# A new order for the first batch's transposes and scores, causal masks on VectorE, and the first v loaded by two queues

## The chip, the cores and the metric

The kernel runs on one core of one Trainium2 chip. The metric is the device time of one execution in microseconds (us). A core has the engines TensorE (PE, matmuls; its weight loads are shown apart as PEld), VectorE (DVE), ScalarE (ACT), GpSimd (POOL) and SyncE (SP), each with its own queue of instructions worked through in order. POOL and SP also issue DMAs.

## The reference

Attention with a decay that each key position carries, then a two-layer feed-forward net with exact GELU on the result.

```python
# q, k, v: (8, 8, 576, 64) float32 (batch, heads, positions, width); s: (8, 8, 576)
scores = scale * np.matmul(q, k.transpose(0, 1, 3, 2))
causal = np.triu(np.ones((S, S), dtype=bool), k=1)
s_pos = np.maximum(s, 0.0)
cum = np.cumsum(s_pos, axis=-1)
bias = -(cum[:, :, :, None] - cum[:, :, None, :])
scores = np.where(causal, -1000000000.0, scores + np.minimum(bias, 0.0))
scores = scores - np.max(scores, axis=-1, keepdims=True)
attn = np.exp(scores)
attn = attn / (np.sum(attn, axis=-1, keepdims=True) + 1e-09)
attn_out = np.matmul(attn, v)
x = attn_out.transpose(0, 2, 1, 3).reshape(B * S, H * D)      # (4608, 512)
h = x @ w_in                                                  # w_in (512, 2048)
out = (0.5 * h * (1.0 + erf(h / np.sqrt(2)))) @ w_out         # w_out (2048, 512)
```

## The kernel before

The work goes by batch b (8 of them, 8 heads each, taken as 4 pairs of heads) and by chunk c of 512 rows of the feed-forward net (9 of them). The scores are computed transposed, keys on the partitions. Since the decay splits into a factor of the key and one of the query, a key's factor (`wb`, an exp of `cum`) is multiplied into v once (`scale_v`, giving `vv`), and numerator and denominator are two matmuls against the same exponentials P.

All instructions of an engine are emitted in the order in which the code below calls them; no scheduler moves them. Waits between engines come from the tiles' reads and writes, and from the number of buffers of a tile. The items:

- `load_pair` issues the q or k of one pair of batch 0, with a cast to bf16, from POOL. `load_v` issues v (ten pieces for batch 0, in two halves of four heads), `load_w` the weights, `load_qk` q and k of a later batch, all from POOL. POOL lets at most eight DMAs be under way: a ninth waits for the first to land. The `pace` copies make POOL wait for a landing or for another engine before it issues more.
- `tr_item(b, p, i)` transposes q (i = 0) or k (i = 1) of a pair: 18 small PE transposes (L350) into one PSUM tile `tr_ps`, then one copy of it into `qkT` (L355), by DVE or, where given, by ACT.
- `sc_item(b, p)` makes the scores of a pair in two units. Each unit is some matmuls (L367) into `sc_ps` and one exp on ACT into P (L383). The causal mask comes in two ways. With `neg=True`, more matmuls add -2048 above the diagonal ahead of the exp (L375, operands `ident_bf` and `neg_bf`). Without it, `mask_item` multiplies P by a triangle of ones and zeros on DVE (L392, L397, operand `tri_bf`).
- `weights_scan`, `weights_dve`, `weights_pe` make `cum` (a scan on DVE, L246) and `wb` (five transposes on PE into `t_ps`, L255, then an exp on ACT).
- `scale_pair(0, p)` makes `vv` of a pair on DVE (L221, two instructions).
- `av_item` makes numerator and denominator of a pair (L405), and `norm` divides by way of ln and exp on ACT (L422, L423) and a product on DVE into `xT` (L438).
- `l1_item` (L486) and `l2_item` (L505) are the two layers.

For batches 0 and 1, q and k are transposed by PE. From batch 2 on DVE interleaves them (`interleave`), SP writes them to DRAM (`write_rows`) and reads them back through the DMA transpose (`transpose_rows`, L185). SP also stores the output (L514).

The prologue, which the change rewrites, works on batch 0. In the kernel before, pair 0 is transposed, then the q of pair 1, then the scores of pair 0; from then on the transposes of a pair come right ahead of its own scores. All four pairs are masked by PE. PE begins with nine matmuls on a tile of zeros (`warm`, L536), and POOL makes the identity after the loads of pair 0. After the prologue come the four `av_item` of batch 0, and then, with c = 0, the feed-forward net with the items of batch 1 between its matmuls.

Of the kernel before, what the change touches and what calls it, by code (L numbers as in the profile page):

```python
# [19 lines left out]
def kernel(  # L20
# [10 lines left out]
    nc = tc.nc  # L31
    fp32 = mybir.dt.float32
    bf16 = mybir.dt.bfloat16
    AF = mybir.ActivationFunctionType
    MULT = mybir.AluOpType.mult
    ALU = mybir.AluOpType
    AX = mybir.AxisListType.X

    B, H, S, D = q.shape
    scale = 1.0 / (D ** 0.5)  # L40
    BH = B * H
    ST = 5
    SL = S - 512
    NP = H // 2
# [38 lines left out]
    work = fast.enter_context(tc.tile_pool(name="work", bufs=1))  # L83
# [10 lines left out]
    early = {}  # L94
# [15 lines left out]
    def load_pair(b, n, p):  # L110
        src = q if n == "q" else k
        if p == 0:
            early[b, n] = work.tile([128, 2, 2, G * D], bf16, tag=f"raw{n}", bufs=3, name=f"early_{n}")
        e0 = (p // 2) * 64
        nc.gpsimd.dma_start(
            out=early[b, n][e0 : e0 + 64, p % 2],
            in_=bass.AP(
                tensor=src.tensor,
                offset=src.offset + (b * H + 2 * p) * S * D,
                ap=[[G * D, 64], [S * D, 2], [1, G * D]],  # L120
            ),
        )

    busy = const.tile([128, 512], bf16, name="busy")
    nc.vector.memset(busy, 0.0)
    for n in "qk":
        load_pair(0, n, 0)
    ident = const.tile([128, 128], fp32, name="ident")
    make_identity(nc, ident)
    for p in range(1, NP):  # L130
        for n in "qk":
            load_pair(0, n, p)
    uptri = const.tile([128, 128], fp32, name="uptri")
# [11 lines left out]
    neg_bf = const.tile([128, 128], bf16, name="neg_bf")  # L145
# [8 lines left out]
    raws = {}  # L154
# [29 lines left out]
        for i in range(2):  # L184
            nc.sync.dma_start_transpose(out=qkT[b % 2][:, i, p, :S], in_=rows_of[b, i][p % 2, p // 2])  # L185

    def load_v(b, h0=0, h1=H):
        if (b, "v") not in raws:
            raws[b, "v"] = work.tile([128, ST, H, D], fp32, tag="rawv", bufs=3, name="raw_v")
        t = raws[b, "v"]  # L190
        for st in range(ST):
            n_st = 128 if st < ST - 1 else SL
            nc.gpsimd.dma_start(  # L193
                out=t[:n_st, st, h0:h1, :],
                in_=bass.AP(
                    tensor=v.tensor,
                    offset=v.offset + (b * H + h0) * S * D + st * 128 * D,
                    ap=[[D, n_st], [S * D, h1 - h0], [1, D]],
                ),
            )  # L200
# [47 lines left out]
    def weights_dve():  # L248
        nc.vector.tensor_scalar(cum, s_pos, s_pos[:, 287:288], None, op0=ALU.subtract)
# [94 lines left out]
    def tr_item(b, p, i, copy=None):  # L344
        t_ps = ps.tile([128, G, 64], bf16, tag="av", bufs=3, name="tr_ps")
        e0 = (p // 2) * 64
        src = early[b, "qk"[i]]
        for r in range(G):
            for e in range(2):
                nc.tensor.transpose(  # L350
                    t_ps[e * 64 : e * 64 + 64, r, :],
                    src[e0 : e0 + 64, p % 2, e, r * D : (r + 1) * D],
                    ident_bf[e0 : e0 + 64, e0 : e0 + 64],
                )
        (copy or nc.vector.tensor_copy)(  # L355
            qkT[b % 2][:, i, p, :S].rearrange("d (g r) -> d g r", r=G), t_ps.rearrange("d r g -> d g r")
        )

    P_of = {}

    def sc_item(b, p, neg=False):
        P_of[b, p] = P = work.tile([128, 2, PW], bf16, tag="P", bufs=4, name="P")
        for u in range(NU):
            s_ps = ps.tile([128, 2, 512], fp32, tag="sc", bufs=2, name="sc_ps")
            for jt, i0, n, off in UNITS[u]:
                for e in range(2):
                    nc.tensor.matmul(  # L367
                        s_ps[:, e, off : off + n],
                        lhsT=qkT[b % 2][e * 64 : e * 64 + 64, 1, p, jt * 128 : jt * 128 + 128],
                        rhs=qkT[b % 2][e * 64 : e * 64 + 64, 0, p, i0 : i0 + n],  # L370
                        start=True, stop=not neg, skip_group_check=neg,
                    )
            for lo, n, w in ((0, 2, 128), (448, 1, 64))[: u + 1 if neg else 0]:
                for e in range(2):
                    nc.tensor.matmul(  # L375
                        s_ps[:, e, 0:512].rearrange("p (g c) -> p g c", c=256)[:, :, 0:128]
                        if n == 2 else s_ps[:, e, lo : lo + w],
                        lhsT=ident_bf,
                        rhs=neg_bf[:, :w].unsqueeze(1).to_broadcast([128, n, w])
                        if n == 2 else neg_bf[:, :w],  # L380
                        start=False, stop=True, skip_group_check=True,
                    )
            nc.scalar.activation(  # L383
                P[:, :, UO[u] : UO[u] + UW[u]], s_ps[:, :, : UW[u]], func=AF.Exp, scale=scale
            )
            if not neg:
                mask_item(b, p, u, nc.vector)

    def mask_item(b, p, u, eng):
        P = P_of[b, p]  # L390
        d = P[:, :, UO[u] : UO[u] + 512].rearrange("p e (g c) -> p e g c", c=256)[:, :, :, 0:128]
        eng.tensor_tensor(  # L392
            d, d, tri_bf.unsqueeze(1).unsqueeze(1).to_broadcast([128, 2, 2, 128]), op=MULT
        )
        if u == 1:
            d = P[:, :, UO[u] + 448 : UO[u] + 512]
            eng.tensor_tensor(  # L397
                d, d, tri_bf[:, :64].unsqueeze(1).to_broadcast([128, 2, 64]), op=MULT
            )
# [123 lines left out]
    def scale_pair(b, p):  # L523
        scale_v(b, ((0, ST - 1), (ST - 1, ST)), nc.vector, 2 * p, 2 * p + 2)

    for t in vv:
        nc.vector.memset(t[64:128, ST - 1, :, :], 0.0)
    make_upper_triangular(nc, uptri, 1.0, diag=True)
    load_v(0, 0, H // 2)
    load_v(0, H // 2, H)  # L530
    for i in range(4):
        load_w(0, i)
    weights_scan()
    warm = ps.tile([128, 2, 512], fp32, tag="sc", bufs=2, name="warm")
    for i in range(9):
        nc.tensor.matmul(warm[:, i % 2], lhsT=busy[:, :128], rhs=busy, start=True, stop=True)  # L536
    tr_item(0, 0, 0, nc.scalar.copy)
    tr_item(0, 0, 1)
    weights_dve()
    nc.vector.tensor_scalar(neg_bf, uptri, 2048.0, -2048.0, op0=MULT, op1=ALU.add)  # L540
    tr_item(0, 1, 0, nc.scalar.copy)
    sc_item(0, 0, neg=True)
    weights_pe()
    tr_item(0, 1, 1)
    sc_item(0, 1, neg=True)
    for p in (2, 3):
        tr_item(0, p, 0)
        tr_item(0, p, 1)
        sc_item(0, p, neg=True)
    nc.vector.tensor_copy(tri_bf, uptri)  # L550
    for p in range(NP):
        scale_pair(0, p)
    nc.gpsimd.memset(amv, 0.0)
    nc.gpsimd.memset(ones, 1.0)
    nc.gpsimd.memset(qkT[1][:, 1, :, S:640], 0.0)
# [121 lines left out]
    with tc.If(rv > 0):  # L677
        with tc.tile_pool(name="gen", bufs=1) as gen, tc.tile_pool(
            name="gps", bufs=1, space=bass.MemoryType.PSUM
# [20 lines left out]
            with tc.For_i(0, B, 1) as b:  # L700
# [8 lines left out]
                for h in range(H):  # L709
# [17 lines left out]
                    for it in range(ST):  # L727
# [27 lines left out]
                        h0 = h - e  # L755
# [68 lines left out]
```

## Time and profile before

| | |
|---|---|
| time, median of 9 runs | 341.92 us (340.9 to 343.35) |
| the profiled execution: its own time, its span | 342.64 us, 340.6 us |
| busy PE, DVE, ACT, POOL | 326.5, 192.5, 203.7, 68.0 us |
| DMA | 47.30 MB, mean 139 GB/s |
| scores of pair 0 start on PE | 8.25 us |
| scores of pair 3 start on PE | 21.74 us |
| first `av_item` starts on PE | 24.01 us |
| first matmul of `l1_item` | 28.82 us |
| first scores of batch 2 | 83.7 us |

The profile is of one execution. In a timeline line the columns are the start in us from the span's start, the duration, the engine, the line of the kernel and the operation, output and inputs, and how many instructions were merged; in brackets stands the engine's idle time just before and what ended it. POOLq and SPq are the instruction queues of those engines, and DMA issues appear on them. A waits line gives the waiting engine and line, what it waited for, and then the total, the number and the longest of the waits. A line of stretches gives, for PE, PEld, DVE, ACT and POOL, the busy time and the number of instructions, and then PEclk (the granted clock), the DMA engines' busy share and GB/s. A line of the chain of waits gives start, duration and what the time went to.

### The profile page before, as it was taken

The page shows a single profiled execution, that of the slowest core. Times are in us where ns is not written, and L with a number is a line of the kernel's source. Part 1 is how long each engine was busy: PE and PEld are TensorE (multiplying, and loading weights), DVE is VectorE, ACT ScalarE, POOL GpSimd, SP SyncE. Part 2 cuts the span into 40 slices and gives each one's busy share as a digit, 9 for nine tenths or more (in the row PEclk, how much of TensorE's full clock was granted, in tenths as well). Part 3 has the DMA queues.
Part 4 walks back from the last instruction along what each step waited for, and adds up shares of the span by engine and source line. Part 5 has one row for each costly group of instructions (what it writes and reads, how often), then busy time and mean ns, then how long its engine had stood idle before and what let it go on. Part 6 is the DMA issues. An engine that isn't in the chain of part 4 may idle for free.

```text
span 340.6 us, 6373 instructions
## 1 busy us (share of the span) xinstructions
PE 326.5 (96%) x2571; PEld 165.3 (49%) x2571; DVE 192.5 (57%) x380; ACT 203.7 (60%) x288; POOL 68.0 (20%) x106
## 2 busy tenths in 40 slices
PE   7889999999999999999999999999999999999992
PEld 3455455554554455445544555455545554444440
DVE  5256638999857655774578456935693455140020
ACT  3549635786767676667756865785578576204400
POOL 8962354410001810070008000500000000000000
PEclk9999999999999999999999999999999999999998
DMA  7899999999477998599688954615710100010011
GB/s 118 187 206 192 205 215 239 206 275 154 137 196 107 192 211 236 130 220 210 158 119 186 202 169 113 178 39 192 126 48 3 62 33 31 33 62 31 3 64 67
DMA packets 53764, 47.30 MB, mean 139 GB/s; under 512 B 31392, under 2 KB 43680, under 8 KB 53728
## 3 DMA queue, kind: packets, MB, share of 16 engines
q0 software_dynamic: 16016, 23.07, 36.8%
q1 hardware_dynamic: 37712, 23.75, 27.7%
q8 instruction: 22, 0.36, 0.4%
q14 instruction: 14, 0.11, 0.1%
HBM read 36.85 MB, written 16.52 MB: 157 GB/s over the span
## 4 chain that ended last, share of the span: by engine, by line
PE 90%; ACT 4%; DVE 2%; DMA 1%; issue 1%; POOL 0%; ACTq 0%; DVEq 0%; POOLq 0%
PE o_ps L505 37%; PE h_ps L486 34%; PE sc_ps L367 6%; PE avn L405 4%; PE avd L405 3%; ACT L492 2%; PE tr_ps L350 1%; PE avw L405 1%; PE sc_ps L375 1%; DMA early_q<-in_q_dram 1%; DVE qkT L355 1%; PE avr L405 1%; ACT gT L492 1%; ACT P L383 1%; PE t_ps L255 0%
## 5 line engine op out<-in xcount | busy, mean ns | idle before, releaser
L505 PE MATMUL o_ps<-w_out_r,gT 128*128 128x512 bf16 x576 | 133.2, 380 | 0.0
L486 PE MATMUL h_ps<-xT,w_in_r 128*128 128x512 bf16 x576 | 126.7, 379 | 1.4 <-ACT gT L492 1.2
L486 PEld LDWEIGHTS <-w_in_r 128*128 128x128 bf16 x576 | 56.2, 98 | 69.9 <-issue 2.9
L383 ACT ACTIVATE P<-sc_ps 128x1024 bf16<-128x1024 f32 x64 | 62.4, 1023 | 39.4 <-PE sc_ps L367 31.7
L505 PEld LDWEIGHTS <-gT 128*128 128x128 bf16 x576 | 52.9, 98 | 60.6
L492 ACT ACTIVATE gT<-h_ps 128x1024 bf16<-128x1024 f32 x54 | 54.4, 1024 | 41.5 <-PE h_ps L486 41.2
L512 DVE COPY o_sb<-o_ps 128x512 f32<-128x512 f32 x36 | 24.8, 688 | 57.3 <-PE o_ps L505 57.3
L392 DVE TENSOR_TENSOR P<-P,tri_bf 128x512 bf16<-128x512 bf16 x56 | 23.6, 425 | 40.1 <-ACT P L383 39.9
L204 DVE TENSOR_REDUCE amx<-qkT 128x2 f32<-128x1152 bf16 x32 | 40.9, 1337 | 0.0
L193 POOL DMA_DIRECT2D raw_v<-in_v_dram x45 | 37.0, 836 | 18.0 <-DMA w_out_r<-in_moe_w_out_dram 7.6
L438 DVE SCALAR_TENSOR_TENSOR xT<-avn,ln 128x256 bf16<-128x256 f32 (+3 forms) x64 | 21.7, 385 | 26.6 <-ACT ln L423 26.6
L367 PE MATMUL sc_ps<-qkT 64*128 64x256 bf16 (+2 forms) x320 | 23.4, 264 | 3.5 <-DVE qkT L355 2.9
L422 ACT ACTIVATE ln<-avd 128x256 f32<-128x256 f32 x56 | 18.6, 393 | 11.1 <-PE avd L405 11.1
L221 DVE TENSOR_TENSOR vv<-raw_v,wb 128x512 bf16<-128x512 f32 (+2 forms) x46 | 25.2, 612 | 0.0
L423 ACT ACTIVATE ln<-ln 128x512 f32<-128x512 f32 (+1 forms) x40 | 23.5, 589 | 1.3
L495 ACT ACTIVATE gT<-h_ps 128x512 bf16<-128x512 f32 x36 | 19.7, 604 | 6.3 <-PE h_ps L486 6.3
L211 DVE TENSOR_REDUCE amv<-raw_v 128x1 f32<-128x2048 f32 (+1 forms) x16 | 22.9, 1471 | 0.0
L367 PEld LDWEIGHTS <-qkT 64*128 64x128 bf16 x320 | 13.3, 96 | 19.5 <-issue 14.6
L405 PEld LDWEIGHTS <-vv 128*64 128x64 bf16 x384 | 17.4, 113 | 6.9 <-issue 3.4
L405 PEld LDWEIGHTS <-wb 128*64 128x64 bf16 x384 | 17.6, 114 | 0.2
L582 POOL CAST pace<-gT 128x1 f32<-128x1 bf16 x4 | 0.8, 199 | 78.5 <-ACT gT L492 78.5
L355 DVE COPY qkT<-tr_ps 128x576 bf16<-128x576 bf16 x14 | 9.9, 752 | 11.5 <-PE tr_ps L350 11.5
(90 smaller groups left out, 177.3 us busy)
## 6 DMA issues: line engine op xcount, KB each, us to landing
out_dram<-o_sb SPq DMA_DIRECT2D x36, 256.0 KB, 2.3
raw_v<-in_v_dram POOLq DMA_DIRECT2D x28, 256.0 KB, 8.4
rows<-qk_bf SPq DMA_DIRECT2D x12, 576.0 KB, 3.4
early_q<-in_q_dram POOLq DMA_DIRECT2D x14, 288.0 KB, 10.4
early_k<-in_k_dram POOLq DMA_DIRECT2D x14, 288.0 KB, 10.5
w_in_r<-in_moe_w_in_dram POOLq DMA_DIRECT2D x4, 512.0 KB, 8.2
w_out_r<-in_moe_w_out_dram POOLq DMA_DIRECT2D x4, 512.0 KB, 14.3
raw_v<-in_v_dram POOLq DMA_DIRECT2D x15, 128.0 KB, 4.8
```

The source lines that it names most:

```text
L193: nc.gpsimd.dma_start(out=t[:n_st, st, h0:h1, :], in_=bass.AP(tensor=v.tensor, offset=v.offset + (b * H + h0) * S * D + st * 128 * D, ap=[ ...
L204: nc.vector.tensor_reduce(amx[:, b * NP + p], qkT[b % 2][:, :, p, :S], axis=AX, op=ALU.max, apply_absolute_value=True)
L221: eng.tensor_tensor(vb[:n_st, st0:st1, h0:h1, :], t[:n_st, st0:st1, h0:h1, :], wb[:n_st, st0:st1, b * H + h0 : b * H + h1] .unsqueeze(3).t ...
L367: nc.tensor.matmul(s_ps[:, e, off : off + n], lhsT=qkT[b % 2][e * 64 : e * 64 + 64, 1, p, jt * 128 : jt * 128 + 128], rhs=qkT[b % 2][e * 6 ...
L383: nc.scalar.activation(P[:, :, UO[u] : UO[u] + UW[u]], s_ps[:, :, : UW[u]], func=AF.Exp, scale=scale)
L392: eng.tensor_tensor(d, d, tri_bf.unsqueeze(1).unsqueeze(1).to_broadcast([128, 2, 2, 128]), op=MULT)
L405: nc.tensor.matmul(out[e * 64 : e * 64 + 64, lo : lo + n], lhsT=(wb[:, jt, b * H + h : b * H + h + 1].to_broadcast([128, 64]) if den else ...
L423: nc.scalar.activation(ln[:, :w], ln[:, :w], func=AF.Exp, scale=-1.0)
L486: nc.tensor.matmul(h_of[c, f2][i], lhsT=w_in_r[:, ko, ft * 128 : (ft + 1) * 128], rhs=xT[:, ko, c * NB % XW : c * NB % XW + NB], start=(ko ...
L492: nc.scalar.activation(gT_of[c][:, f2 * 2 : f2 * 2 + 2, :], hh_of[c, f2], func=AF.Gelu)
L505: nc.tensor.matmul(o_ps, lhsT=gT[:, ft, sub * 128 : (sub + 1) * 128], rhs=w_out_r[:, ft, :], start=(ft == 0), stop=(ft == FT - 1),)
L512: nc.vector.tensor_copy(o_sb, o_ps)
```

## The change

The transposes of a pair are emitted ahead of the scores of the pair in front of it, so that the k of pair p + 1 and the q of pair p + 2 stand on PE between two score items. Pairs 0, 1 and 2 are no longer masked by matmuls: `mask_item` on DVE does it, after the last of the transposes' copies and between the scalings of v; pair 3 keeps `neg=True`. q and k of pair 1 are issued ahead of the identity, which moves the identity on POOL behind two more DMA issues. The first four heads of v are issued by SP, the others by POOL; a small POOL copy from `early_k` (pair 1) into the v tile stands ahead of both, so that v is issued after that k has landed. One of the nine warm-up matmuls goes, and `neg_bf` and `tri_bf` are made later on DVE.

```diff
-    for n in "qk":
-        load_pair(0, n, 0)
+    for p in (0, 1):
+        for n in "qk":
+            load_pair(0, n, p)
     ident = const.tile([128, 128], fp32, name="ident")
     make_identity(nc, ident)
-    for p in range(1, NP):
+    for p in (2, 3):
         for n in "qk":
             load_pair(0, n, p)
...
-    def load_v(b, h0=0, h1=H):
+    def v_tile(b):
+        raws[b, "v"] = work.tile([128, ST, H, D], fp32, tag="rawv", bufs=3, name="raw_v")
+
+    def load_v(b, h0=0, h1=H, eng=nc.gpsimd):
         if (b, "v") not in raws:
-            raws[b, "v"] = work.tile([128, ST, H, D], fp32, tag="rawv", bufs=3, name="raw_v")
+            v_tile(b)
...
-            nc.gpsimd.dma_start(
+            eng.dma_start(
...
-    def sc_item(b, p, neg=False):
+    def sc_item(b, p, neg=False, masks=True):
...
-            if not neg:
+            if masks and not neg:
                 mask_item(b, p, u, nc.vector)
...
-    load_v(0, 0, H // 2)
+    v_tile(0)
+    nc.gpsimd.tensor_copy(
+        raws[0, "v"][:64, :, 0, 0], early[0, "k"][:64, 1, 0, 0:1].to_broadcast([64, ST])
+    )
+    load_v(0, 0, H // 2, nc.sync)
     load_v(0, H // 2, H)
...
-    for i in range(9):
+    for i in range(8):
         nc.tensor.matmul(warm[:, i % 2], lhsT=busy[:, :128], rhs=busy, start=True, stop=True)
     tr_item(0, 0, 0, nc.scalar.copy)
     tr_item(0, 0, 1)
     weights_dve()
-    nc.vector.tensor_scalar(neg_bf, uptri, 2048.0, -2048.0, op0=MULT, op1=ALU.add)
     tr_item(0, 1, 0, nc.scalar.copy)
-    sc_item(0, 0, neg=True)
+    sc_item(0, 0, masks=False)
     weights_pe()
     tr_item(0, 1, 1)
-    sc_item(0, 1, neg=True)
-    for p in (2, 3):
-        tr_item(0, p, 0)
-        tr_item(0, p, 1)
-        sc_item(0, p, neg=True)
+    tr_item(0, 2, 0)
+    nc.vector.tensor_scalar(neg_bf, uptri, 2048.0, -2048.0, op0=MULT, op1=ALU.add)
+    sc_item(0, 1, masks=False)
+    tr_item(0, 2, 1)
+    tr_item(0, 3, 0)
     nc.vector.tensor_copy(tri_bf, uptri)
+    sc_item(0, 2, masks=False)
+    tr_item(0, 3, 1)
+    mask_item(0, 0, 0, nc.vector)
+    mask_item(0, 0, 1, nc.vector)
+    sc_item(0, 3, neg=True)
     for p in range(NP):
         scale_pair(0, p)
+        if p < 2:
+            mask_item(0, p + 1, 0, nc.vector)
+            mask_item(0, p + 1, 1, nc.vector)
```

## The prediction

> **What bounds the kernel now.** I read the page first, then the chain of waits for the first 45 us, the waits of TensorE (PE), the timeline of each engine there, and last the DMA landings.
>
> ```profile
> PE   7889999999999999999999999999999999999992
> PE 90%; ACT 4%; DVE 2%; DMA 1%; issue 1%; POOL 0%; ACTq 0%; DVEq 0%; POOLq 0%
> ```
>
> PE is the bound: 90% of the chain that ends last, and short of nine tenths only in the first three slices, some 25 us. From L1's start at 28.8 us on it hardly waits, so a microsecond taken from the prologue reaches the end, unless a later wait eats it. The timeline, PE alone:
>
> ```profile
> 8.25 0.61 PE L367 MATMUL sc_ps<-qkT 64*128 64x256 bf16 x4
> 8.79 0.61 PE L375 MATMUL sc_ps<-neg_bf,ident_bf 128*128 128x256 bf16 x2
> 9.33 0.61 PE L367 MATMUL sc_ps<-qkT 64*128 64x256 bf16 x6
> 9.87 0.72 PE L375 MATMUL sc_ps<-neg_bf,ident_bf 128*128 128x256 bf16 x4
> 10.52 0.79 PE L255 MATMUL t_ps<-ident,cum 64*128 64x64 f32 x5
> ...
> 15.05 0.69 PE L350 MATMUL tr_ps<-ident_bf,early_q 64*64 64x64 bf16 x18
> 15.55 0.67 PE L350 MATMUL tr_ps<-ident_bf,early_k 64*64 64x64 bf16 x18
> 17.26 0.61 PE L367 MATMUL sc_ps<-qkT 64*128 64x256 bf16 x4 [1.04 <-DVE qkT L355]
> ...
> 21.74 0.61 PE L367 MATMUL sc_ps<-qkT 64*128 64x256 bf16 x4 [1.04 <-DVE qkT L355]
> ...
> 24.01 0.96 PE L405 MATMUL avw<-P,vv 128*64 128x256 bf16 x8
> ```
>
> Two things are seen: masks (L375) cost as much PE time as scores, and PE stands still while DVE copies the transposes it needs next. The waits of PE and the chain add the wait for pair 1's q:
>
> ```profile
> PE sc_ps L367 <- DVE qkT L355: 2.9, 3, 1.0
> ...
> 3.13 4.46 DMA early_q<-in_q_dram
> ```
>
> The second limit is the loads (timeline, all engines):
>
> ```profile
> 7.25 7.23 POOL L193 DMA_DIRECT2D raw_v<-in_v_dram  x10
> ...
> 14.46 3.01 POOL L238 DMA_DIRECT2D w_in_r<-in_moe_w_in_dram  x4
> ```
>
> and, in the stretches of 2 us, the DMA share (last but one) falls while POOL issues without a pause:
>
> ```profile
> 8.00:10.00 2.00, 2.00 (x25) 0.86 (x22) 0.06 (x1) 1.21 (x2) 2.00 (x4) 1.00 1.18 202
> 12.00:14.00 2.00, 1.22 (x8) 0.40 (x10) 0.73 (x1) 0.05 (x2) 2.00 (x4) 1.00 0.69 170
> 18.00:20.00 2.00, 2.00 (x30) 1.19 (x30) 0.00 (x0) 1.39 (x2) 0.00 (x0) 1.00 1.24 201
> ```
>
> From 18 us the share stays near 1.24: the DMA engines are full. The backlog reaches batch 2, whose first scores PE starts at 83.7 us:
>
> ```profile
> 73.72 7.36 SPq L185 DMA_TRANSPOSE qkT<-rows  x4
> ```
>
> The first of these takes 7.9 us to land, the second (issued at 76.94) 5.2, hence 82.1: only 1.6 us ahead of PE. This is where a faster prologue can be lost.
>
> **The change part by part, PE.** *Start.* POOL issues pair 1's q and k (0.60 + 0.62 us) ahead of the identity. q1 leaves 0.53 us earlier (3.13 to 2.60), so I take its landing at 7.05 instead of 7.58 and its transposes done at 7.8. In exchange the identity's cast on DVE slips from 3.21 to 4.42, and with it the scan queued behind (1.28 us later, 1.35 long): 7.05. The copy of k0, behind the scan, ends at 7.81. Pair 0's transposes wait for nothing new (q0 lands at 1.25 + 3.4 = 4.65, when the cast ends too; the ninth warm-up matmul removed, 0.43 us, was in their way). Scores of pair 0: 7.86 instead of 8.25; between 0 and 0.45 gained, I take 0.4.
>
> *Masks off PE.* Start to start, L375 costs 0.54 + 0.65 = 1.19 us a pair; three pairs, 3.57 us.
>
> *Order.* Before, 8.25 to 21.74 is 13.49: three score items at 2.27 (6.81), weights 0.72, transposes 0.64 + 2 x 1.14 (2.92), and 3.04 of standing still. After, with the same durations (score item 1.08; two transposes 1.14; the DVE copy 0.76, starting 0.69 after its first transpose; 0.05 to hand over): scores 0 at 7.86; weights 8.94; k1, q2 from 9.67 to 10.81; k1 copied 11.11; scores 1 at 11.16; k2, q3 12.24 to 13.38; k2 copied 13.69; scores 2 at 13.74; k3 14.82 to 15.46, copied 16.27; scores 3 at 16.3. Standing still falls to 0.35 + 0.36 + 0.86 = 1.57, as the copy outlasts the one transpose beside it. Gain at scores 3: 21.74 - 16.3 = 5.44 us, the start's 0.4 in it. ACT keeps up: two exps of 1.03 in a period of 2.6.
>
> *DVE.* From 16.27 come three masks and four scalings. A mask is two L392 (mean 0.425) and one L397 (0.22): 1.07 end to end, 0.81 start to start (60.66, 61.00, next at 61.13); I take 0.95. A scaling is 3.29 / 4 = 0.82. v of pairs 0 to 3 is ready at 18.0, 19.8, 21.6, 22.4; PE wants it at 18.6, 20.1, 21.55, 22.5. At 1.07 the last two come 0.4 and 0.25 late. I charge 0.1: gain 5.35. This cover is gone if DVE runs late, microsecond for microsecond. neg_bf (0.53) and tri_bf (0.22) fall between copies while DVE waits for PE.
>
> *Clock.* The page's PEclk is full throughout, yet eight matmuls of L405 take 0.75 us from 24.01 and 0.39 from 27.57: PE speeds up 5.4 us after it last stood still (21.74). The Trainium skill, TensorE: Matmul & The Clock Gate (Part 1), says full clock comes after a busy window of some 3.4 us that runs free, so 3.4 to 6.8 us after 16.3. By the row the sum is unchanged; by the rule it is up to 0.7 worse, or 0.2 better (v of pair 3 holds the rest). I keep 0 and put both in the range.
>
> **Loads.** POOL loses five v issues to SP: 7.23 / 2 = 3.62. But its first v now stands behind a small copy that waits for k1's landing (7.8, at worst 8.3 as before), which SP waits for too; with 0.2 for the copy (L556's is 0.18) POOL restarts at 7.5 to 8.1 instead of 7.25, or 8.5 at worst. w_in leaves at 11.1 to 11.7, not 14.46: D = 2.8 to 3.3, I take 3.0. Behind it w_out and all later loads shift alike, as pace waits for w_in. SP's half meanwhile shares engines with q2 to k3: half of v is 0.59 MB, 2.2 us at the 268 GB/s of the stretch 10 to 12. q3 landed by 10.7 (q1's 7.6 and four steps of some 0.75, the spacing of q1 and k1), now 0.5 earlier: at worst 12.4, and PE wants it at 12.7; k3 13.2 against 14.8. v itself, landed by about 15, is not wanted before 17.2. SP's queue is free until 47 us.
>
> Here a rule speaks against the change. DMA: Bandwidth & Descriptors (Issuing engines are not separate DMA queues) says queues share the same 16 engines, and issuing from several saves only issue time. By it alone D = 0. The trace shows that issue time is what lacks: share 0.69 with POOL at 2.00 of 2.00. I take 3.0.
>
> **Sum.** PE comes to batch 2's scores 5.35 earlier, their transposes land 3.0 earlier with 1.6 of slack: a stall of 0.75 if the landing follows the backlog, none if it follows its issue (rows are written earlier too). I take 0.5. Net 4.85. The profiled execution lasted 342.64 (span 340.60 and 2.04 around it): 337.8. The median shown, 341.92, is 0.72 below that execution: **337.1 us**.
>
> **Rivals.** *Loads do not move (D near 0).* For: the full DMA share from 18 us, the rule. Against: the dip from 12 to 18. Then batch 2's scores wait to 82.1 as before: net 1.6, 340.3.
>
> *DVE becomes the bound* in 16 to 23 us: its 6.1 us of queue against PE's 6.2. If masks or copies cost a quarter more beside POOL's issuing, 1 to 1.5 us is lost ahead of the stall, whose 0.5 then goes: net 4.1, 337.8. For: no slack at v2. Against: L392 beside POOL issues at 62.5 us took its usual 0.43.
>
> *Slower: the transposes of batch 2 land later than 83.7.* SP's stores and rows now start 5 us earlier and meet more of POOL's backlog; rows already took 9.3 us and a transpose 7.9. If this moves p0's landing from 82.1 beyond 83.7, each further us is a loss: at 85.5 it is 1.8, 343.7. Against: the bytes are the same and start earlier.
>
> *It does not do what it says*: k1 lands late enough (over 10 us) that POOL and SP wait away the 3.6 gained. Then the loads shift by nothing: 340.3. Unlikely, as it landed by 8.3.
>
> **How the numbers follow.** The forecast has 0.65, own range 336.2 to 338.4 (start 0 to 0.45, clock +0.7 or -0.2, stall 0 to 1). DVE as the bound 0.15; loads that do not move 0.10 (net 0.7 to 3); POOL and SP waiting it away 0.02 (again 340.3); late transposes 0.08, of which 0.01 ends within 0.2%. A difference below 0.2%, 0.7 us, cannot be told from none. Faster 0.92, same 0.01, slower 0.07. The range runs from 336.2 to 340.2: it leaves out the late transposes, part of the loads' case and the lower edge.
>
> **What would show it.** Right: L375 in pair 3 alone; scores of pair 3 at 16.3, av at 18.6, L1 at 23.4; w_in issued near 11.4; a wait of PE under 1 us at batch 2's first scores. Wrong: PE waiting there for 2 us or more (the loads), PE L405 waiting for DVE (the masks), or scores 0 after 8.2 (the identity).

## The result and the profile after

The changed kernel takes **337.58 us** (median of 10 runs, 336.45 to 339.29) against 341.9 us (31 runs of the kernel before beside it): a ratio of **0.988 [0.986, 0.990]**, 4.3 us less. The prediction was 337.1 us, range 336.2 to 340.2. The first profiled execution of the changed kernel lasted 340.05 us (span 338.2), longer than any of its timed runs, so a second profile of the same kernel (338.76 us, span 336.8) stands beside it below.

The page of the first, its row of busy tenths and its chain of waits by engine:

```profile
PE   7779999999999999999999999999999999999992
PE 87%; DMA 4%; ACT 4%; DVE 1%; POOL 1%; issue 1%; SPq 1%; DVEq 0%; ACTq 0%; POOLq 0%
```

PE still bounds the kernel; DMA's share of the chain has gone from 1% to 4%. The timeline of PE in the first execution, where before the scores of pair 3 started at 21.74 and the first matmul of L1 at 28.82 (line numbers are 4 higher than before: L371 scores, L379 masks, L409 av, L490 first layer):

```profile
15.85 0.61 PE L371 MATMUL sc_ps<-qkT 64*128 64x256 bf16 x4 [0.85 <-DVE qkT L359]
16.39 0.61 PE L379 MATMUL sc_ps<-neg_bf,ident_bf 128*128 128x256 bf16 x2
...
18.11 0.96 PE L409 MATMUL avw<-P,vv 128*64 128x256 bf16 x8
...
21.52 0.96 PE L409 MATMUL avw<-P,vv 128*64 128x256 bf16 x8 [1.70 <-DVE vv L225]
...
26.26 4.06 PE L490 MATMUL h_ps<-xT,w_in_r 128*128 128x512 bf16 x15
```

The scores of pair 3 start 5.9 us earlier and are the only ones with mask matmuls. Then PE waits 1.70 us for v of pair 1, and L1 has gained only 2.56. DVE's timeline names what was late:

```profile
19.77 0.28 DVE L225 TENSOR_TENSOR vv<-raw_v,wb 64x128 bf16<-64x128 f32 x1 [2.04 <-DMA raw_v<-in_v_dram]
```

It is the last piece of SP's half of v, issued at 10.32 and landed 9.36 us later (the chain of waits), at 19.7:

```profile
10.32 9.36 DMA raw_v<-in_v_dram
```

In the second execution the same piece took 7.3 us. PE's timeline has no wait for v there; instead PE stands before the first scores of batch 2:

```profile
15.66 0.61 PE L371 MATMUL sc_ps<-qkT 64*128 64x256 bf16 x4 [0.86 <-DVE qkT L359]
...
22.95 2.97 PE L490 MATMUL h_ps<-xT,w_in_r 128*128 128x512 bf16 x11
...
80.08 0.61 PE L371 MATMUL sc_ps<-qkT 64*128 64x256 bf16 x10 [2.03 <-DMA qkT<-rows]
```

L1 gained 5.87 us here, and PE would have come to batch 2 at 78.05; its transposes landed at 80.0 (before: 82.1). So two executions of one kernel lose part of the gain in different places, and the loads are behind both.

POOL and SP in the first execution, to set beside the 7.23 us of ten v issues and the w_in issue at 14.46 before:

```profile
8.10 3.67 POOL L197 DMA_DIRECT2D raw_v<-in_v_dram  x5
8.18 4.70 SPq L197 DMA_DIRECT2D raw_v<-in_v_dram  x5
11.73 2.29 POOL L242 DMA_DIRECT2D w_in_r<-in_moe_w_in_dram  x3
14.70 0.74 POOL L242 DMA_DIRECT2D w_in_r<-in_moe_w_in_dram  x1 [0.69 <-DMA raw_v<-in_v_dram]
```

w_in leaves 2.7 us earlier. Its fourth piece waits until a piece of v has landed: eight DMAs of POOL, five of v and three of w_in, are under way by then.

### The profile page after: what moved, and what is told of

Its sections match the earlier page's. It is cut to its first block, busy times and chain, and to the rows that moved or that the text cites. A ratio compares the mean times of both kernels' runs of the same rounds, so it can differ in the third digit from the quotient of the medians.

```text
span 338.2 us, 6355 instructions
## 1 busy us (share of the span) xinstructions
PE 324.1 (96%) x2552; PEld 164.8 (49%) x2552; DVE 194.5 (58%) x389; ACT 203.2 (60%) x288; POOL 65.8 (19%) x102
## 4 chain that ended last, share of the span: by engine, by line
PE 87%; DMA 4%; ACT 4%; DVE 1%; POOL 1%; issue 1%; SPq 1%; DVEq 0%; ACTq 0%; POOLq 0%
PE o_ps L509 37%; PE h_ps L490 35%; PE sc_ps L371 5%; PE avn L409 4%; PE avd L409 3%; DMA raw_v<-in_v_dram 3%; ACT L496 2%; DMA early_k<-in_k_dram 1%; PE avr L409 1%; ACT gT L496 1%; ACT P L387 1%; PE avw L409 1%; PE tr_ps L354 1%; SPq L197 1%; POOL early_q L115 0%
## 5 line engine op out<-in xcount | busy, mean ns | idle before, releaser
L490 PE MATMUL h_ps<-xT,w_in_r 128*128 128x512 bf16 x576 | 127.1, 380 | 1.2 <-ACT gT L496 1.2
L490 PEld LDWEIGHTS <-w_in_r 128*128 128x128 bf16 x576 | 56.4, 98 | 70.1 <-issue 3.4
L396 DVE TENSOR_TENSOR P<-P,tri_bf 128x512 bf16<-128x512 bf16 x62 | 25.8, 423 | 40.0 <-ACT P L387 39.8
L197 POOL DMA_DIRECT2D raw_v<-in_v_dram x40 | 33.5, 854 | 14.7 <-DMA w_out_r<-in_moe_w_out_dram 6.9
L371 PE MATMUL sc_ps<-qkT 64*128 64x256 bf16 (+2 forms) x320 | 22.9, 265 | 2.4 <-DVE qkT L359 1.8
L371 PEld LDWEIGHTS <-qkT 64*128 64x128 bf16 x320 | 13.8, 98 | 17.5 <-issue 13.4
L409 PEld LDWEIGHTS <-vv 128*64 128x64 bf16 x384 | 17.5, 114 | 9.2 <-issue 3.4
L409 PEld LDWEIGHTS <-wb 128*64 128x64 bf16 x384 | 18.1, 117 | 0.4
L409 PE MATMUL avn<-P,vv 128*64 128x256 bf16 x224 | 16.8, 275 | 0.0
L409 PE MATMUL avd<-P,wb 128*64 128x256 bf16 x224 | 16.2, 269 | 0.0
```

The costliest lines, as they stand in the source:

```text
L197: eng.dma_start(out=t[:n_st, st, h0:h1, :], in_=bass.AP(tensor=v.tensor, offset=v.offset + (b * H + h0) * S * D + st * 128 * D, ap=[[D, n_ ...
L371: nc.tensor.matmul(s_ps[:, e, off : off + n], lhsT=qkT[b % 2][e * 64 : e * 64 + 64, 1, p, jt * 128 : jt * 128 + 128], rhs=qkT[b % 2][e * 6 ...
L396: eng.tensor_tensor(d, d, tri_bf.unsqueeze(1).unsqueeze(1).to_broadcast([128, 2, 2, 128]), op=MULT)
L409: nc.tensor.matmul(out[e * 64 : e * 64 + 64, lo : lo + n], lhsT=(wb[:, jt, b * H + h : b * H + h + 1].to_broadcast([128, 64]) if den else ...
L490: nc.tensor.matmul(h_of[c, f2][i], lhsT=w_in_r[:, ko, ft * 128 : (ft + 1) * 128], rhs=xT[:, ko, c * NB % XW : c * NB % XW + NB], start=(ko ...
```

## The experiments

The question was which of the two limits sets the gain, and which of the three parts (order, masks, split) pays. All in one table: the time, the ratio to the kernel before run beside it, then from one profiled execution when L1 starts, when PE was ready for the first scores of batch 2 (their start less the wait for `qkT<-rows`), and when they started. A profile is one execution and need not be a typical one: those of `split_only` and `v_all_pool` took 343.24 and 343.48 us, 2.0 and 1.9 above the medians. The masks alone, without order and split, were not run.

| kernel | median us | ratio | L1 | PE ready | start |
|---|---|---|---|---|---|
| before | 341.9 | | 28.82 | 83.72 | 83.72 |
| changed, first | 337.58 | 0.988 [0.986, 0.990] | 26.26 | 81.39 | 81.39 |
| `after_again` | 337.65 | 0.989 [0.986, 0.991] | 22.95 | 78.05 | 80.08 |
| `v_swap` | 336.83 | 0.986 [0.984, 0.988] | 23.11 | 78.38 | 78.61 |
| `v_all_pool` | 341.60 | 0.998 [0.996, 1.000] | 22.40 | 78.71 | 81.96 |
| `fill` | 338.11 | 0.991 [0.988, 0.994] | 23.06 | 78.33 | 78.72 |
| `split_only` | 341.24 | 0.997 [0.995, 0.999] | 29.77 | 84.48 | 84.48 |
| `pe_masks` | 340.21 | 0.995 [0.993, 0.997] | 26.94 | 81.54 | 81.54 |
| `v_all_pool_late` | 338.33 | 0.990 [0.987, 0.992] | 22.56 | (scores moved) | 81.05 |
| `v_swap_late` | 337.16 | 0.985 [0.983, 0.988] | 23.34 | (scores moved) | 80.25 |
| `masks_only` | 337.88 | 0.990 [0.987, 0.993] | 22.99 | 78.25 | 78.88 |
| `no_copy` | 337.35 | 0.987 [0.984, 0.991] | 23.80 | 78.91 | 78.91 |
| `ident_first` | 336.89 (one run) | | 23.59 | 78.21 | 78.21 |
| `w_in_held` | 347.71 (one run) | | 27.96 | 85.11 | 87.44 |

Two regularities carry the rest. From L1's start to PE being ready for batch 2 it is 54.6 to 55.3 us in every row but `v_all_pool` (56.3) and `w_in_held` (57.2). From the start of those scores to the end of the span it is 256.6 to 256.9 in every row but `v_all_pool` (259.6), `w_in_held` (258.4) and the two where the scores were moved. In the two that stand apart PE ran at half clock for a part of this time (below), and in `v_all_pool` it also waited 0.7 us for w_out. So, of what changes between the profiled executions, **the time is the later of "L1 + 55" and "the transposes' landing", plus a constant.**

**The same kernel again** (`after_again`, no edit), to see whether the wait for v belongs to the change.

> The changed kernel once more, beside the three others on the same chip. In its first profile PE reached the av item of pair 0 5.9 us earlier than before, then stood 1.7 us for v of pair 1, whose half came from SP and landed at 19.7 us, and was still at half speed at 26 us. If that wait belongs to the kernel, it comes again here within 0.5 us (v of pair 1 ready at 21 to 22, a wait of PE of 1.2 to 2.2 us at av of pair 1). If it was an accident of that execution, v lands by 16 us and PE does not wait. Time against before: 0.988 either way, the earlier interval being 0.986 to 0.990.

Shown above: no wait for v, L1 at 22.95, a wait of 2.0 us at batch 2. The wait for v is not in every execution.

**The other half by SP** (`v_swap`): the heads wanted first are issued by POOL.

```diff
-        raws[0, "v"][:64, :, 0, 0], early[0, "k"][:64, 1, 0, 0:1].to_broadcast([64, ST])
+        raws[0, "v"][:64, :, H // 2, 0], early[0, "k"][:64, 1, 0, 0:1].to_broadcast([64, ST])
-    load_v(0, 0, H // 2, nc.sync)
-    load_v(0, H // 2, H)
+    load_v(0, H // 2, H, nc.sync)
+    load_v(0, 0, H // 2)
```

> SP issues the heads of pairs 2 and 3, POOL those of pairs 0 and 1; nothing else differs from the changed kernel. Theory A (the loss between 18 and 26 us is the wait for SP's half of v, and the half clock that its pause prolongs): pairs 0 and 1 now land with POOL's half by 17.5 us, PE does not wait at av of pair 1, SP's half still lands at 19 to 20 and pair 2 wants it at about 21, so at most 0.3 us of wait is left; L1 starts 1.5 to 3 us earlier than 26.3; time 0.7 to 2 us below the changed kernel's, a ratio to before of 0.982 to 0.986. Theory B (the clock alone, which comes when it comes; the wait only lies inside slow matmuls' time): L1 starts at most 0.5 us earlier, same ratio as the changed kernel within 0.001. Theory C (what is gained is lost again at the loads of batches 1 and 2): L1 starts earlier, but PE waits for loads later and the ratio does not move.

It has the lower median, by 0.8 us, but the interval overlaps that of the changed kernel. PE does not wait for v (DVE does, 0.8 us), and waits 0.2 us at batch 2. That v's order costs something on average is not shown.

**All of v by POOL** (`v_all_pool`): order and masks without the split.

```diff
-    load_v(0, 0, H // 2, nc.sync)
+    load_v(0, 0, H // 2)
     load_v(0, H // 2, H)
```

> All of v issued by POOL again, first half first, in the changed kernel; the copy that waits for k of pair 1 stays. Theory A: POOL's v moves in packets of 4 KB and the first half lands by 15 us, no wait at av of pair 1, L1 1.5 to 3 us earlier than 26.3; w_in leaves at about 15.3 instead of 11.7 but its first piece lands at most 1 us later than 20.2, as it did not gain by leaving early; ratio to before 0.982 to 0.987. My prediction's loads term (POOL freed of five issues moves all later loads 3 us ahead): w_in lands 2 to 3 us later than in the changed kernel, and PE pays up to 1 us for it at batch 2; ratio about 0.990.

This is the miss that decided the case. If SP's late half of v were the main loss, this kernel had to be the fastest; L1 does start earliest of all, at 22.40, and nearly nothing is left of it: 0.998 [0.996, 1.000]. The timelines of SP and PE:

```profile
68.23 10.77 SPq L186 DMA_TRANSPOSE qkT<-rows  x4
...
81.96 1.04 PE L371 MATMUL sc_ps<-qkT 64*128 64x256 bf16 x10 [3.25 <-DMA qkT<-rows]
```

The transposes land at 81.9, as before the change (82.1), although the first is issued 5.5 us earlier (68.23 against 73.72): it is not their issue that holds them. PE waits. Its stretches of 2 us show a second price (the clock PEclk is the third from the end):

```profile
80.00:82.00 2.00, 0.04 (x2) 0.04 (x4) 1.91 (x2) 0.28 (x1) 0.00 (x0) 0.80 1.30 121
82.00:84.00 2.00, 1.67 (x12) 0.99 (x14) 0.33 (x1) 1.39 (x2) 0.00 (x0) 0.50 1.19 317
84.00:86.00 2.00, 2.00 (x6) 0.71 (x5) 0.65 (x3) 0.55 (x1) 0.00 (x0) 0.50 0.56 118
86.00:88.00 2.00, 2.00 (x6) 0.50 (x4) 0.00 (x0) 0.00 (x0) 0.00 (x0) 0.50 0.20 41
88.00:90.00 2.00, 2.00 (x37) 1.57 (x37) 1.76 (x4) 1.44 (x2) 0.00 (x0) 0.99 0.10 38
```

Near the end of 3.2 us of standing still the clock fell to half, for some 6.8 us, which can account for the 2.8 us by which this row exceeds the constant. But this execution took 343.48 us, 1.9 above the median (the runs go from 338.13 to 343.53), so this second price is not shown for the others. The wait of 2.0 us in `after_again` was not followed by half clock; one of 2.3 us in `w_in_held` was (PEclk 0.50 from 88 to 90 us, 0.67 from 90 to 92).

**The wait's place** (`v_all_pool_late`, `v_swap_late`): more of the second layer's matmuls, 12 and 8 instead of 4, ahead of batch 2's first scores.

```diff
-            l2_item(c, 0, 0, 4)
+            m = 12 if c == 1 else 4
+            l2_item(c, 0, 0, m)
             sc_item(nb, 0)
-            l2_item(c, 0, 4)
+            l2_item(c, 0, m)
```

> The kernel with all of v issued by POOL, and in addition batch 2's first scores placed behind 12 instead of 4 of the matmuls of the first output tile at c = 1, 1.7 us later on PE; no other difference. In the former PE waited 3.2 us at these scores for the DMA transposes, with the clock at half for 6.8 us afterwards. Theory D: transposes still land at 82 us, the wait shrinks to about 1.5 us and the half-speed stretch goes with it or shortens; 1.5 to 4.5 us less than that kernel, ratio to before 0.985 to 0.994. Rival (the gain of the order goes somewhere else without the split, for instance at w_out, where PE waited 0.7 us, or spread over the loads of batch 1): within 0.8 us of that kernel, ratio 0.996 to 1.000.

> The kernel in which SP issues the later half of v, and in addition batch 2's first scores behind 8 instead of 4 matmuls of the first output tile at c = 1, 0.86 us later on PE. Theory D: PE's wait there was 0.2 us in the profile, so 0.2 us are to be had where it comes early, and up to 1 us in executions in which the transposes land later; ratio 0.983 to 0.986 against 0.9863 without. Rival: no wait is left to be taken and av of batch 2 has to wait for the later exp; ratio 0.987 to 0.989.

With the wait filled, order and masks alone come from 0.998 to 0.990 [0.987, 0.992]: the wait was 0.9 us, the landing itself 0.9 us earlier, and no half clock followed.

```profile
81.05 0.61 PE L371 MATMUL sc_ps<-qkT 64*128 64x256 bf16 x10 [0.87 <-DMA qkT<-rows]
```

So most of the gain of `v_all_pool` had been lost at this one place. With the split (`v_swap_late`, 0.985) nothing more is seen to be had: it is not told apart from `v_swap`.

**The split alone** (`split_only`): the kernel before, v split over SP and POOL behind the small copy.

```diff
-    load_v(0, 0, H // 2)
+    raws[0, "v"] = work.tile([128, ST, H, D], fp32, tag="rawv", bufs=3, name="raw_v")
+    nc.gpsimd.tensor_copy(
+        raws[0, "v"][:64, :, 0, 0], early[0, "k"][:64, 1, 0, 0:1].to_broadcast([64, ST])
+    )
+    load_v(0, 0, H // 2, nc.sync)
     load_v(0, H // 2, H)
```

> The kernel before with nothing changed but v of batch 0: first half by SP, second by POOL, both behind the small copy. Theory D (the change needs two things at once: the order gives PE 5 to 6 us, the split brings the transposes of batch 2 to land at 78.6 to 80 us instead of 82.1, and the smaller of the two is what is gained): w_in leaves 2.5 to 3 us earlier, k of batch 2's pair 0 lands 2 to 3.5 us earlier, at 78.6 to 80, but PE comes to its scores at 83.7 as before and has no use for it; v is wanted at 21.7 only, SP's half lands by 20: ratio to before 0.998 to 1.002. Rival: the split is itself worth 2 us or more, because PE is served better somewhere; ratio 0.994 or less.

```profile
84.48 0.78 PE L367 MATMUL sc_ps<-qkT 64*128 64x256 bf16 x10
```

PE waits for nothing there; the transposes had landed at 79.4 (issue time plus the time to landing in the DMA view), 2.7 us earlier than before, where PE does not need them. 0.997 [0.995, 0.999]. By what way that 0.3% comes is not shown: the profiled execution, 2.0 us above the median, waits 2.5 us for pair 1's q (1.3 before) and reaches L1 and batch 2 later than the kernel before. The split alone is worth 0.3%, order and masks without it 0.2%, hardly told from nothing; together they are worth 1.2%.

**Order without masks** (`pe_masks`): the changed kernel with `neg=True` for all pairs and no `mask_item` in the prologue.

```diff
-    sc_item(0, 0, masks=False)
+    sc_item(0, 0, neg=True)
...
-    mask_item(0, 0, 0, nc.vector)
-    mask_item(0, 0, 1, nc.vector)
     sc_item(0, 3, neg=True)
```

> The changed kernel with the masks of pairs 0 to 2 back on PE (neg=True for all four, no masks on DVE; neg_bf made ahead of the scores of pair 0). Counting by my prediction: three times 1.19 us more on PE, scores of pair 3 start at 19.4 instead of 15.8 (up to 0.5 less where the longer scores cover the waits for copies), the gain at L1 is 2.3 to 2.8 us, batch 2's transposes land at 78.6 to 80 and PE comes at about 81: no wait there. Theory D: ratio 0.992 to 0.994, so of the changed kernel's 4 us about half is the masks' and half the order's. Rival (DVE's masks cost what they save, since vv comes later by them): ratio as the changed kernel's, 0.988.

The scores of pair 3 start at 19.49, between 21.74 and 15.66. L1 follows at 26.94, PE is ready at 81.54, the transposes were there at 80.2: PE's own gain of 2.2 us is kept whole, as the formula has it. The ratio, 0.995 [0.993, 0.997], falls a little short of the 0.992 to 0.994 expected. The median is 1.0 us below that of `split_only`, beside which it ran, though the two intervals overlap: with the masks on PE the order seems to be worth some 0.3%.

**Masks without order** (`masks_only`): `split_only`, with the masks on DVE, before's order of transposes and scores, before's identity, nine warm-up matmuls.

```diff
-    sc_item(0, 0, neg=True)
+    sc_item(0, 0, masks=False)
...
-        sc_item(0, p, neg=True)
+        sc_item(0, p, neg=p == 3, masks=False)
     nc.vector.tensor_copy(tri_bf, uptri)
+    mask_item(0, 0, 0, nc.vector)
+    mask_item(0, 0, 1, nc.vector)
     for p in range(NP):
         scale_pair(0, p)
+        if p < 2:
+            mask_item(0, p + 1, 0, nc.vector)
+            mask_item(0, p + 1, 1, nc.vector)
```

> The kernel before with the v split over SP and POOL, and with the masks of pairs 0, 1 and 2 on DVE between the scalings, but with before's order of transposes and scores, before's place of the identity and nine warm-up matmuls. If a mask pair costs PE 1.19 us of matmuls (working of the prediction), three are 3.57 us less: scores of pair 3 start at 18.2 to 19 instead of 22.5 (split alone) , L1 at about 25.5 to 26.3, and since the transposes of batch 2 land at 78.6 to 80.2, ahead of the 80.3 at which PE then comes to its scores, nearly all of it is kept: ratio 0.987 to 0.990, as good as the whole change, and the order would pay next to nothing. If the order is what removes the standing still and the matmuls of masks filled time in which PE waited for DVE's copies anyway, scores of pair 3 start at 19.5 or later and the ratio is 0.991 to 0.995.

The ratio, 0.990 [0.987, 0.993], is that of the first theory and not told apart from the whole change; the steps on the way are of neither. PE stands still as long as before (2.9 us, the waits of PE), yet the scores of pair 3 start at 16.15, earlier than either theory had them:

```profile
PE sc_ps L367 <- DVE qkT L355: 2.9, 3, 1.0
...
7.59 0.61 PE L367 MATMUL sc_ps<-qkT 64*128 64x256 bf16 x10
...
16.15 0.61 PE L367 MATMUL sc_ps<-qkT 64*128 64x256 bf16 x4 [1.04 <-DVE qkT L355]
...
21.23 0.57 PE L405 MATMUL avn<-P,vv 128*64 128x256 bf16 x8 [0.50 <-DVE vv L221]
...
22.99 0.38 PE L486 MATMUL h_ps<-xT,w_in_r 128*128 128x512 bf16 x1
```

Part of that is the clock: eighteen transposes took 0.69 us at 5.15 and 0.47 at 7.18, the ten matmuls of pair 0's scores 0.61 against 1.03 in the first profile of the changed kernel, and only between 9 and 10 us does PEclk fall to half. `ident_first` below, with the new order and as fast there (0.47 and 0.61), starts the scores of pair 3 at 14.62, 1.5 us earlier, which is the difference of standing still for the copies (2.9 against 1.4), and L1 at 23.59, 0.6 later. Two things lie between. The scalings: in six profiles (`after_again`, `v_swap`, `fill`, `masks_only`, `no_copy`, `ident_first`) DVE begins the first at 16.5 to 17.4, in four of them after a wait for v, and ends the last at 22.0 to 22.3, whatever the order on PE; L1 follows 0.8 to 1.5 us later. And the clock: PE was at full clock from about 19.8 in `masks_only` and from about 22.6 in `ident_first`. So the new order's 1.5 us is real at the scores and was not found at L1, where v's landing, DVE's scalings and the clock decide. How much is due to each of these is not separated. For the question of which part pays it means: masks and split together bring what the whole change brings, as far as these intervals can tell, and that the order adds to them is not shown.

**Filling PE behind pair 0** (`fill`): four matmuls on zeros behind the first `av_item`.

```diff
         av_item(0, p, wide=p < 2, rest=False, last=p == 3)
+        if p == 0:
+            fill = ps.tile([128, 512], fp32, tag="mlp", bufs=1, name="fill")
+            for i in range(4):
+                nc.tensor.matmul(fill, lhsT=busy[:, :128], rhs=busy, start=True, stop=True)
```

> Four more matmuls of 512 columns on zeros (1.7 us at half speed) after the av item of pair 0 in the changed kernel, where PE waits 1.7 us for v of pair 1; they keep PE busy and compute nothing that is used. If the pause itself puts off full speed (theory A's second part): PE reaches full speed 5 to 6 us after 15.85, at 21 to 22, not at 27.6, the wait for v stays hidden under the four, L1 starts about 1 to 1.5 us earlier, time 0.5 to 1.5 us less than the changed kernel's. If a pause of 1.7 us does not matter to the clock: L1 starts where it did or, where the wait is shorter, up to 1 us later, and the time is the same or up to 0.5 us more.

0.991 [0.988, 0.994], not told apart from the changed kernel. The clock was full from 18.7, early, and L1 started at 23.06, no earlier than in `after_again`, whose clock was full only from 21.6. An earlier clock gained nothing here, where the scalings ended at 22.25.

**v without its copy** (`no_copy`): the POOL copy ahead of v removed, so that SP issues from 1.4 us and no queue waits for k of pair 1.

```diff
-    nc.gpsimd.tensor_copy(
-        raws[0, "v"][:64, :, 0, 0], early[0, "k"][:64, 1, 0, 0:1].to_broadcast([64, ST])
-    )
```

> The changed kernel without the small POOL copy ahead of v: SP issues its half of v from about 1.5 us, POOL its half as soon as it has issued k of pair 3 and finished the triangle. If the copy protects q and k of pairs 1 to 3 from v on the shared engines, q1 and k1 land 1 us or more later, scores of pair 0 start at 8.5 us or later instead of 7.73, scores of pair 3 at 16.5 or later, and the ratio is 0.990 or more. If there is room on the engines in the first 8 us, SP's half of v has landed by 15, no wait for v, scores of pair 3 stay at 15.7 to 15.9, and with weights leaving earlier the ratio is 0.984 to 0.988.

The first theory is right on the front: q of pair 1 is transposed at 8.25 instead of 7.07, the scores of pair 0 start at 8.65, those of pair 3 at 16.76. The loss of time that it expected, a ratio of 0.990 or more, is not seen: 0.987 [0.984, 0.991]; PE comes to batch 2 at 78.91 and waits for nothing. The copy does protect q and k; here the delay cost nothing that could be measured.

**The identity back in front** (`ident_first`), one run.

```diff
-    for p in (0, 1):
-        for n in "qk":
-            load_pair(0, n, p)
+    for n in "qk":
+        load_pair(0, n, 0)
     ident = const.tile([128, 128], fp32, name="ident")
     make_identity(nc, ident)
-    for p in (2, 3):
+    for p in (1, 2, 3):
```

> The changed kernel with the identity back between the loads of pair 0 and those of pair 1. By the prediction q of pair 1 then leaves POOL 0.5 us later and lands 0.5 later, and scores of pair 0 start at 8.1 to 8.3 us instead of 7.73, scores of pair 3 at 16.1 to 16.3 instead of 15.7 to 15.9. If the start hangs on the scan on DVE and the copy of k0 instead, the earlier identity lets scores of pair 0 start as early or earlier, 7.7 or below.

```profile
3.12 0.60 POOL L115 DMA_DIRECT2D early_q<-in_q_dram  x1
...
6.98 0.47 PE L353 MATMUL tr_ps<-ident_bf,early_q 64*64 64x64 bf16 x18 [1.10 <-DMA early_q<-in_q_dram]
7.38 0.61 PE L370 MATMUL sc_ps<-qkT 64*128 64x256 bf16 x10
```

q of pair 1 leaves 0.5 us later than in the changed kernel and lands no later (its transposes at 6.98 against 7.07 and 6.96), and the scores of pair 0 start at 7.38, earlier than 7.73. The second theory holds in this execution: the moved identity bought nothing. `after_again` shows the wait for the copy of k0 behind the transposes of q1:

```profile
7.73 0.84 PE L371 MATMUL sc_ps<-qkT 64*128 64x256 bf16 x10 [0.30 <-DVE qkT L359]
```

**w_in held back** (`w_in_held`), one run: POOL issues w_in only after SP's half of v has landed.

```diff
+    held = const.tile([64, 1], fp32, name="held")
+    nc.gpsimd.tensor_copy(held, raws[0, "v"][:64, ST - 1, 0, 0:1])
+    nc.gpsimd.tensor_copy(w_in_r[:64, 0, 0:1], held)
```

> The changed kernel with w_in held back on POOL until the last piece of SP's half of v has landed (two small copies, from that piece into a scratch tile and from there into the tile of w_in). In the changed kernel SP's half landed at 19.7 and 17.6 us in two executions, although issued by 13. If it is late because w_in's packets share the engines with it, it lands by 16 here and w_in leaves at about 16 instead of 11.7, with no wait of TensorE for v. If SP's small packets are slow by themselves, it still lands after 17 and w_in leaves only then; L1 may then wait for w_in.

```profile
8.17 4.45 SPq L197 DMA_DIRECT2D raw_v<-in_v_dram  x5
17.63 0.32 POOL L540 COPY held<-raw_v 64x1 f32<-64x1 f32 x1 [5.87 <-DMA raw_v<-in_v_dram]
18.01 4.16 POOL L541 CAST w_in_r<-held 64x1 bf16<-64x1 f32 x1
22.46 3.00 POOL L242 DMA_DIRECT2D w_in_r<-in_moe_w_in_dram  x4 [0.30 <-POOL w_in_r L541]
```

SP's half still lands only at 17.5, with nothing of w_in in the queues: w_in's packets are not what makes it land at 17 and a half, though they may be behind the 19.7 of the one execution. That is the number of the second theory, but its reason, small packets, is not shown. The DMA views of `w_in_held` and, last line, of `v_all_pool` (issuing queue, count, size, us from issue to landing) give the last, smaller piece of a half:

```profile
raw_v<-in_v_dram SPq DMA_DIRECT2D x1, 64.0 KB, 7.2
raw_v<-in_v_dram POOLq DMA_DIRECT2D x1, 64.0 KB, 6.2
...
raw_v<-in_v_dram POOLq DMA_DIRECT2D x1, 64.0 KB, 2.6
```

POOL's half, issued up to 11.1, is as late as SP's: it lands at 17.3. Where POOL issues all of v alone, a piece takes 2.4 to 3.7 us, the first half has landed by 14.2 and the second by 17.6.

w_in left 10.7 us later than in the changed kernel (4.16 of it in the second small copy, which was not meant), and the time went to 347.7. Most of that was lost at L1, ahead of batch 2 (PE's timeline):

```profile
27.96 2.29 PE L490 MATMUL h_ps<-xT,w_in_r 128*128 128x512 bf16 x5 [4.17 <-issue]
```

The first piece of w_in landed at 27.9, and PE ran at half clock until about 33. At batch 2, whose transposes landed at 87.4, it waited 2.3 us more. So delayed loads of the prologue do reach batch 2, but here they cost more on the way.

## Why the prediction was right

**The two limits** were the core of it, and both were found: "PE comes to batch 2's scores 5.35 earlier, their transposes land 3.0 earlier with 1.6 of slack". PE was ready 5.7 us earlier in `after_again` (78.05 against 83.72) and 2.3 in the first profile; the landing moved from 82.1 to 80.0 and 78.9. The stall, taken as 0.5, was 2.0 and 0. What the sum had as one case, a full gain of PE and a small stall, the two executions shared out differently. Two of the signs of being wrong that the prediction had named did appear, one in each execution: "PE waiting there for 2 us or more" (2.03 in `after_again`) and PE's av waiting for DVE (1.70 in the first profile, though for v, not for the masks). The sum, 4.85 us, measured 4.3. That it came so near is in part luck: v came later than counted and the order paid less at L1, while L1 came near its forecast even without the new order (22.99 in `masks_only`).

**Masks off PE**, 3.57 us: from `pe_masks` to `after_again` the scores of pair 3 move from 19.49 to 15.66, 3.8 us, of which 0.2 is the start of pair 0's scores (7.95 and 7.73). The term is right at the scores.

**Order.** Standing still from 3.04 to 1.57: the waits of PE for `qkT` of pairs 1 to 3 sum to 1.8 in both profiles. The scores of pair 3 were put at 16.3 and came at 15.66 to 15.85. The term is right at the scores, but the prediction carried it through to L1, and `masks_only` has none of it there (22.99 against 22.95). The rival "DVE becomes the bound" has the mechanism, in that the end of the scalings leads L1, but not its price: the last scaling ended at 22.0 to 22.3 where the forecast itself had 22.4, and L1 came at 23 where it had 23.4. Its sum hid the overlap, since it already let L1 follow v's readiness and left 0.1 between PE and DVE.

**Start**, 0.4: the scores of pair 0 came 0.5 earlier, but not for the reason given. "q1 leaves 0.53 us earlier ... so I take its landing at 7.05": `ident_first` has the later issue and the same landing. The other leg of the same working, the copy of k0 that ends at 7.81, is what PE waited for in `after_again`.

**"v itself, landed by about 15, is not wanted before 17.2"** is the step that failed. SP's half landed at 17.5 to 17.8 in `after_again`, `w_in_held` and `ident_first`, and at 19.7 in the first profile. The only working near it divided the bytes of SP's half, 0.59 MB, by the bandwidth of a stretch. POOL's half, as many bytes, was under way at the same time and landed no sooner than 17.3 to 17.6. The two halves were interleaved: all of v had landed at about 17.6 in `v_all_pool` as well, but there the half that is wanted first came first, by 14.2. A second thing was left out. The page shows that the issuing engine changes the packets: those under 512 B, 31392 before, are now

```profile
DMA packets 55925, 47.30 MB, mean 140 GB/s; under 512 B 33697, under 2 KB 45985, under 8 KB 55889
```

2305 more, about one for each of the 2304 rows of 256 B in SP's half. All packets together are only 2161 more (53764 before, and 53765 in `v_all_pool`), so that some 144 larger ones went: 0.59 MB in 144 packets is 4 KB each, which is how POOL's queue had moved the same rows. Whether twice the bytes under way or the smaller packets make the pieces of both halves slow, no run separates. Nor is it known what held SP's last piece until 19.7 in the first profile, where POOL's half had landed by 17.4; there PE waited 1.7 us and reached full clock only at 27.6.

**Loads.** D = 3.0 was put together as an earlier issue carried through. The issue moved as forecast (w_in at 11.73, 2.7 us earlier), but w_in's first piece landed no earlier (20.24 against 19.95), since issue to landing grew from 5.5 to 8.5 us. Without the split it is later still: in `v_all_pool`, where POOL waits for k1 too and issues all of v, w_in leaves at 15.75 and its first piece lands at 21.6. The gain is seen further down the stream: batch 2's transposes landed between 77.8 and 80.2 in all profiles with the split but `w_in_held`, and at 81.0 and 81.9 in the two without. "DMA: Bandwidth & Descriptors" of the Trainium skill (Issuing engines are not separate DMA queues) says that issuing from several engines saves only issue time, usually a small thing, and the prediction read D = 0 from it. Here issue time was what lacked, as the dip in DMA share had said: the runs with and without the split differ by 0.8 to 4.1 us at batch 2's landing. By what way the gain reaches batch 2 was not followed.

**Clock**, kept at 0: from PE's last standing still to full clock it was 5.6 us before (21.74 to 27.4), and after the change 3.4 (`fill`), 3.7 (`v_all_pool`), 5.2 (`v_swap`), 5.9 (`after_again`) and 6.1 (first profile, from 21.52). This agrees with the 3.4 to 6.8 us that the prediction cited, and it varies from kernel to kernel: a term with that spread could not be set to one number. `ident_first` fits less well: full clock came 8.1 us after its last wait for a copy (14.62), with pauses of 0.3 and 0.7 us between, and 3.1 us after the later of these.

## What to carry to other kernels

Before a prologue is made shorter, look for the next transfer that PE will meet early, and measure the slack: here the split, worth 0.3% alone, and order with masks, worth 0.2% and hardly told from nothing, were worth 1.2% together, since each lifted one of two limits. A pause of PE can be charged twice, as the wait and as the half clock after it (3.2 and 2.3 us were, 2.0 us was not, one execution each); filling it with matmuls that stood behind it was worth 0.8%, two thirds of what the whole change brought. When a load is moved to another issuing engine, count all that is under way beside it, and look at its packet sizes on the page as well as at the issue time. And run the parts of a change in pairs: masks and split without the new order came out as the whole.

## What was not expected of the hardware

A POOL copy of one element per partition (the `pace` copy, which releases the issue of w_out) takes 0.18 us in the kernel before, while DVE is idle. Next to the masks and scalings it waits through several of DVE's instructions, often to the end of their run. POOL's timelines of `no_copy`, `masks_only` and `v_all_pool`, and the last scalings of `no_copy` and `masks_only` on DVE:

```profile
18.21 4.16 POOL L568 CAST pace<-w_in_r 128x1 f32<-128x1 bf16 x1 [3.34 <-DMA w_in_r<-in_moe_w_in_dram]
20.65 1.68 DVE L225 TENSOR_TENSOR vv<-raw_v,wb 128x512 bf16<-128x512 f32 x4
```

```profile
20.09 2.14 POOL L565 CAST pace<-w_in_r 128x1 f32<-128x1 bf16 x1 [4.77 <-DMA w_in_r<-in_moe_w_in_dram]
20.50 1.68 DVE L221 TENSOR_TENSOR vv<-raw_v,wb 128x512 bf16<-128x512 f32 x4
```

```profile
21.64 0.18 POOL L571 CAST pace<-w_in_r 128x1 f32<-128x1 bf16 x1 [2.34 <-DMA w_in_r<-in_moe_w_in_dram]
```

It began at 18.21 and at 20.09, and ended at 22.37 and 22.23, each time when the scalings ended (22.33 and 22.18); in `v_all_pool` it began just after them and took 0.18. It does not always wait for the whole run: in the first profile it began at 20.30 and ended at 21.72, when the scalings of pair 1 ended (21.67), with more masks and scalings still to come. The page "SBUF — State Buffer" of the Trainium skill (SBUF: two separate sides) describes a lock: a DVE instruction with two SBUF inputs and a POOL instruction that reads SBUF share a pair of ports, and the loser waits. The runs show more, a wait through several DVE instructions in a row. DVE's work thus held up POOL's next issue by up to 4 us. That the runs show no loss by it does not prove that it cost nothing; the rest of w_in was still on its way.
